# One V of each layer split by rows over five DMA engines: a two-layer decode kernel on one Trainium2 core

## Chip, core and metric

The kernel runs on one core of one Trainium2 chip. The metric is the device time of one execution in microseconds (us), as the median of the runs. Before the change it is 511.55 us, over 3 runs from 511.38 to 511.69.

## What is computed

One token of 640 numbers goes through two layers, and both layers use the same weights and the same caches:

```
x = x + A(layernorm(x))       # attention of one query over the last 4096 keys
x = x + B(layernorm(x))       # a mixer: two steps with a GELU in between
...
def A(x):
    q = (x @ wq).reshape(32 heads, 192)
    scores = q . k[last 4096 keys] * 192 ** -0.5        # per head
    p = softmax(scores)
    o = p . v[last 4096 keys]                           # per head, 192 numbers
    return o.reshape(6144) @ wo
```

Each of the 32 heads has a K and a V of 4096 x 192 bf16 numbers, 1.5 MB each, in HBM. (Of the reference's mixer B, the kernel computes what its output needs with one token.)

## The kernel before

**Layout.** A head's K or V lies in SBUF as 128 partitions of 32 keys each: partition p has the keys 32p to 32p + 31 in one row of 12,288 bytes. The 32 places in a row are called key blocks here. SBUF holds twelve such tiles, the cells (`take` and `give`, L147 to L153), and a few smaller places: `kx` (14 key blocks wide), `kl` (10), `wx_sb`, `wq_sb`.

**The stream of loads.** `layer_stream` (L247) writes down the order of all loads by hand, and `need` (L291) issues them on SP's queue in that order, in the place where the program first asks for a later one. In the steady part the K of the next group of four heads and the V of the present group take turns, and a part of `wo` follows each group. Layer 0 takes the groups from the last heads to the first, layer 1 from the first to the last. Some heads' data stay in SBUF between the layers: the transposed K of heads 0 to 7, and the V of heads 2, 3 and part of 4. `kx` and `kl` hold parts of the V of head 4 from late in layer 0 until its use early in layer 1. After a layer's attention the mixer's weights W3 and W4 are loaded (`load_w3` L212, `load_w4` L224). SP waits before an issue until the cell is free and until the semaphore that the load will use is free again; eight semaphores go round.

**How a load is split.** A load runs on up to 16 DMA engines. `load_wide` (L49) reads four rows at a time, so that a K or V is 32 packets of 49,152 bytes, two for each engine. The plain form makes a packet of each row, eight for each engine.

**The work on a head.** `T` turns K on DVE (L450), `S` makes the scores on PE (L534). Per group `softmax_steps` (L551) makes the weights of all four heads and turns them, so that `PT` (L607) has the weight of key block j of partition p in row p. `pv` (L645) multiplies: 16 products of two key blocks each (L654), added up in four strips of PSUM; DVE then turns the sums (L661), and `o_fold` (L663) adds them up. `give` in `pv` (L660) frees the cell. The products with `wo` are added up in rows, `acc` and `q_row`, for which `row_space` (L424) picks a place: in layer 1 the start of `kx`.

**Ends of layers.** In the mixer, L1015 makes the products with W3 and L1062 those with W4; the layer's result needs both. Layer 1 begins with scores of the kept heads, which need no load. Its first loads (L156, at 281.7 and 289.5 us of the span) wait for cells that the end of layer 0 frees.

Of the kernel before, what the change touches and what calls it, by code (L numbers as in the profile page):

```python
# [10 lines left out]
F32 = mybir.dt.float32  # L11
U32 = mybir.dt.uint32
ACTF = mybir.ActivationFunctionType
ALU = mybir.AluOpType
AX = mybir.AxisListType
# [3 lines left out]
P = 128  # L19
# [13 lines left out]
NJ4, NGK, NM = 4, 8, 4  # L33
# [22 lines left out]
        name=nc.get_next_instruction_name(), ins=sym[:1], outs=sym[1:], queue="qSPDynamicHW", mode="Copy"))  # L56


@with_exitstack
def kernel(  # L60
    ctx: ExitStack,
# [13 lines left out]
    nc = tc.nc  # L75
    shrink_ring(nc)
    _, _, D = A_x.shape
    _, H, Sk, Dh = A_k_cache.shape
# [9 lines left out]
    QH = 4  # L88
# [5 lines left out]
    FREE = NT * QUART  # L94
    scale = float(Dh) ** -0.5
    eps = 1e-5
    s0 = Sk - W

    NA = Dh // 32
    NKX, NKL = 14, 10  # L100
# [5 lines left out]

    VC, VP, VX, VW, VN = 3, 2, 4, 20 * Dh // 2, (NKL + NKX) * Dh
    assert NA * D + FREE - 2 * VW <= FREE

    W3C, W4C = FREE // F, FREE // D  # L110
    assert W4C % 2 == 1 and NF - W4C == 3
# [6 lines left out]
    kl = low.tile([P, NKL * Dh], BF16, name="kl")  # L118
# [9 lines left out]
    psm = ctx.enter_context(tc.tile_pool(name="psm", bufs=2, space=PSUM))  # L128
# [5 lines left out]
        name=nc.get_next_instruction_name(), act_func_set_id=ACT_TABLE_SET, ins=[], outs=[]))  # L134

    wq_sb = fixed.tile([P, ND, HD], BF16, name="wq_sb")
    wx_sb = fixed.tile([P, (ND - W3C) * F + (NF - W4C) * D], BF16, name="wx_sb")

    kx = fixed.tile([P, NKX * Dh], BF16, name="kx")
# [7 lines left out]
    def take(key):  # L147
        i = free.popleft()
        cell_of[key] = i
        return (low if i == NCELL - 1 else cells).tile([P, FREE], BF16, tag=f"cell{i}", name=f"cell{i}")  # L150

    def give(key):
        free.append(cell_of.pop(key))  # L153

    def load(dst, src, wide=True):
        (partial(load_wide, nc) if wide else nc.sync.dma_start)(dst, src)  # L156
# [10 lines left out]
        return t  # L167

    def load_v(layer, h):
        t = take(("v", layer, h))  # L170
        src = A_v_cache[0, h, s0:Sk, :].rearrange("(p j) d -> p (j d)", p=P)
        cut = (2 * VW,) if h == VP else (FREE - VN, FREE - NKX * Dh) if h == VX else ()
        if h in GROUPS[layer][-1][-1 - layer:]:
            cut = FREE // 2,
        i = 0
        for e in cut + (FREE,):
            kept_v = h == VP or h == VX and i > 0
            if not cut:
                load(t[:], src, layer == 0 or h >= 2)
            elif layer == 0 or not kept_v:  # L180
                nc.sync.dma_start(v_pair(t, h, i, e - i), src[:, i:e])
            i = e
        return t

    def v_pair(V, h, i, n):
# [105 lines left out]
    def need(*key):  # L291
        while key not in loaded:
            k = stream[pos[0]]
            pos[0] += 1
            loaded[k] = LOADERS[k[0]](*k[1:])
        return loaded[key]
# [3 lines left out]
    ident = const.tile([P, P], F32, name="ident")  # L300
# [3 lines left out]
    o_sb = big.tile([P, 2, NA, 32], F32, name="o_sb")  # L304
# [3 lines left out]
    def column(n):  # L308

        i = used[0]  # L310
        used[0] += n
        return words[:, i:i + n]
# [12 lines left out]
    def short_bf16(name, n, bufs=1):  # L325
        return short(name, (n + 1) // 2, bufs).bitcast(BF16)[:, 0:n]
# [3 lines left out]
        out=ident[:], in_=ident[:], compare_op=ALU.not_equal, fill=1.0,  # L330
# [7 lines left out]
    for base in (0, -1, -64, -65):  # L338
        nc.gpsimd.affine_select(
            out=Lf, in_=Lf, compare_op=ALU.not_equal, fill=1.0,  # L340
# [6 lines left out]
    Ei = ident[:].bitcast(BF16).rearrange("p (c two) -> p c two", two=2)[:, :, 1]  # L347
# [12 lines left out]

    Lq = head.tile([P, 32], F32, name="Lq")
    nc.vector.reduce_sum(Lq[:], ident[:].rearrange("p (j a) -> p a j", j=4), axis=AX.X)
    eps1 = column(1)
    nc.vector.memset(eps1[:], eps)

# [8 lines left out]
    QAT = 0, QPAIR, QPAIR + 2 * NM, NM  # L374
    Qblk = const.tile([P, 2, QSLOT], BF16, name="Qblk")
    nc.gpsimd.memset(Qblk[:], 0.0)


    warm_ps = psm.tile([32, 32], F32, tag="psm")
    for i in range(WARM):  # L380
# [9 lines left out]
                            op1=ALU.add, accum_out=rs0[:, 0:1])  # L390
# [32 lines left out]

    def row_space(layer):  # L424

        t, i = ((wx_sb, 8 * P), (kx, 0))[layer]
        return t[0:33, i:i + D].bitcast(F32), t[0:33, i + D:i + D + QC // 2]

    kept = {}
# [201 lines left out]
    O_ps = O_bank[:, 0:2 * Dh]  # L631
# [3 lines left out]
    def v_words(layer):  # L635

        V = need("v", layer, VP)
        step = 512
        for i in range(0, VW, step):
            n = min(step, VW - i)  # L640
            a = V[:, 2 * i:2 * (i + n)].bitcast(U32)
            b = V_bank[:, i:i + n].bitcast(U32)
            nc.vector.transpose(b if layer == 0 else a, a if layer == 0 else b)  # L643

    def pv(layer, h, hq, PT, mid=None):  # L645
        V = need("v", layer, h)
        if (layer, h) == (0, VP):
            v_words(0)
        NB = NJ4 * NGK // 2
        for i in range(NB):  # L650
            if mid is not None and i == NB // 2:
                mid()
            r = 32 * (i % 4)
            nc.tensor.matmul(O_ps[r:r + 2, :], lhsT=PT[:, hq, 2 * i:2 * i + 2],  # L654
                             rhs=v_pair(V, h, 2 * i * Dh, 2 * Dh), start=(i < 4), stop=(i >= NB - 4))
        if (layer, h) == (0, VC):
            loaded["v", 1, h] = V
            cell_of["v", 1, h] = cell_of.pop(("v", 0, h))
        else:
            give(("v", layer, h))  # L660
        nc.vector.transpose(o_sb[:], O_ps.rearrange("p (e a c) -> p e c a", e=2, c=NA))  # L661
# [64 lines left out]
    def attention(layer, x_cur, rs_cur, x_new, z_new, rs_new, ss_new):  # L726
# [54 lines left out]
        def center_y():  # L781
            y.pop()()
# [25 lines left out]
        early = None  # L808

        acc, q_row = row_space(layer)  # L810
        rows = range(2 * layer, len(groups) - 3 + layer)

# [6 lines left out]
        for gi, cur in enumerate(groups):  # L819
# [4 lines left out]
            quick = hurry and layer == 1  # L824
            ST_n = None
            if nxt:
# [3 lines left out]
                if layer == 1 and gi == 0:  # L830
# [17 lines left out]
                    PT = swap()  # L848
# [4 lines left out]
                else:  # L853
# [19 lines left out]
                    if layer == 1:  # L873
                        turn_p()
                        PT = swap()
# [16 lines left out]
                    if layer == 0:  # L892
                        PT = swap()
# [5 lines left out]
            else:  # L899
                PT, rl = early  # L900
            oT = short_bf16("oT", NA, 2)
            fold = None
            order = list(enumerate(cur))
            if layer == 1 and gi == 0:
                order.insert(0, order.pop(cur.index(VC)))
            for hq, h in order:
                if quick and hq == 1:
                    (q2, h2), (q3, h3) = nxt
                    T(h2, 0)
                    T(h2, 1)  # L910
                elif quick and hq == 2:
                    T(h3, 1)
                elif layer == 1 and nxt and 0 < hq < 3:
                    T(nxt[0][1], 0)
                pv(layer, h, hq, PT, steps[3] if quick and hq == 3 else fold)
                if final:
                    if hq == 0:
                        add_y(out_proj(layer, pending) if layer == 0 else turn_row(acc), 1)
                    if hq == 1:
                        center_y()  # L920
                    fold = None
                    if hq < QH - 2:
                        o_fold(h, oT, rl)
                    else:
                        def fold(h=h):
                            o_fold(h, oT, rl)

                    continue
                if quick and hq == 1:
                    S(h2, 0, ST_n, q2)  # L930
                    S(h2, 1, ST_n, q2)
                    T(h3, 0)
                elif quick and hq == 2:
                    S(h3, 0, ST_n, q3)
                    o_fold(h, oT, rl)
                    S(h3, 1, ST_n, q3)
                    steps = softmax_steps(len(cur), ST_n, sc, kl[:].bitcast(F32), V_bank)
                    for step in steps[:3]:
                        step()
                    continue  # L940
                elif hurry and hq == 1:
                    (q2, h2), (q3, h3) = nxt
                    for half in range(2):
                        T(h2, half)
                        S(h2, half, ST_n, q2)
                    T(h3, 0)
                    S(h3, 0, ST_n, q3)
                    T(h3, 1)
                elif hurry and hq == 2:
                    S(h3, 1, ST_n, q3)  # L950
                    steps = softmax_steps(len(cur), ST_n, sc, o_words)
                    steps[0]()
                    steps[1]()
                elif nxt and not (hurry and hq == 3):
                    q2, h2 = nxt.pop(0)
                    for half in range(2):
                        T(h2, half)
                        S(h2, half, ST_n, q2)
                o_fold(h, oT, rl, len(groups) - 4 > gi >= 2 * layer)
                if hurry and hq == 3:  # L960
                    for step in steps[4 if quick else 2:5]:
                        step()
                    early = steps[5](), steps[6]()
# [154 lines left out]
```

## Time and profile before

| | |
|---|---|
| median of 3 runs | 511.55 us |
| profiled execution | 511.54 us |
| its span, first to last instruction | 509.7 us |
| PE, DVE, ACT, POOL busy | 61%, 57%, 10%, 1% of the span |
| bytes moved by DMA | 214.63 MB, 421 GB/s on average |
| chain that ended last: share of DMA | 60% |
| a V's load, from issue to landing (median) | 27.7 us |

The profile is of one execution. The span leaves out what lies around it, here 1.8 us, so a change of so many us in the span is one of as many in the time. In the chain, each piece is what the next one waited for, followed back from the end. In groups of instructions the columns are the line, the engine, the operation, what it writes and reads, the shapes and the number, then busy us and the mean ns of one, then the idle time before them and who ended it. A queue's row has packets, megabytes and the share of 16 engines' time that the packets took.

### The profile page before, as it was taken

Reading aid. Unit: us, or ns where it says so; the run is one execution under the profiler, and the core shown is the slowest. Engines: PE = TensorE matmul, PEld = TensorE weight load, DVE = VectorE, ACT = ScalarE, POOL = GpSimd, SP = SyncE. Lnnn points to the kernel's source line nnn. Section 1 sums busy time; section 2 is a strip of 40 time slices with the busy share of each in tenths; the row PEclk is TensorE's granted clock in tenths of the full one; section 3 lists DMA queues with packets and bytes.
Section 4 is the critical chain, followed back from the end, with each engine's and each line's share of the span. In section 5 each row is a group of like instructions: output and inputs, shape, how many; then the busy total and the mean of one; then the engine's idle time right before and its main releaser. Section 6 shows DMA issues by size and latency. Waiting matters only on the chain.

```text
span 509.7 us, 9498 instructions
## 1 busy us (share of the span) xinstructions
PE 313.2 (61%) x4084; PEld 186.2 (37%) x4084; DVE 292.6 (57%) x604; ACT 48.9 (10%) x173; POOL 3.7 (1%) x16
## 2 busy tenths in 40 slices
PE   1056667666565555857655766767655765557685
PEld 0023333343332322534333643544322433324354
DVE  2067557666674755566723244968666656656522
ACT  1000101010010100001010101010100101001101
POOL 2000000000000000000000000000000000000000
PEclk9999756777597766576765586789887766857655
DMA  8999999999999999999999999999999999999996
GB/s 370 432 432 429 430 441 432 429 429 422 417 426 441 432 425 446 432 402 458 429 391 413 381 438 424 439 429 429 426 429 433 429 430 432 418 437 429 418 409 250
DMA packets 12014, 214.63 MB, mean 421 GB/s; under 512 B 2564, under 2 KB 3076, under 8 KB 7428
## 3 DMA queue, kind: packets, MB, share of 16 engines
q1 hardware_dynamic: 11972, 214.02, 98.5%
q8 instruction: 32, 0.52, 0.4%
q14 instruction: 10, 0.08, 0.0%
HBM read 214.01 MB, written 0.00 MB: 420 GB/s over the span
## 4 chain that ended last, share of the span: by engine, by line
DMA 60%; PE 20%; DVE 14%; issue 4%; ACT 1%; SPq 1%; DVEq 0%; ACTq 0%
DMA cell<-in_A_k_cache_dram 37%; DMA cell<-in_A_v_cache_dram 19%; DVE cell L450 9%; PE ST_ps L534 9%; PE O_ps L654 5%; DMA cell<-in_B_w_dram 4%; DVE o_sb L661 2%; PE qT_ps L480 1%; PE y_ps L1062 1%; PE nb_ps L580 1%; DVE words L557 1%; PE l_ps L613 1%; DVE V_ps L643 1%; DVE o_sb L591 1%; SPq L55 0%
## 5 line engine op out<-in xcount | busy, mean ns | idle before, releaser
L534 PE MATMUL ST_ps<-cell,Qblk 128*16 128x256 bf16 x1536 | 157.8, 364 | 110.8 <-DVE cell L450 66.6
L450 DVE STREAM_TRANSPOSE cell<-cell 128x768 uint32<-128x768 uint32 x224 | 201.6, 946 | 33.7 <-DMA cell<-in_A_k_cache_dram 31.6
L534 PEld LDWEIGHTS <-Qblk 128*16 128x16 bf16 x1536 | 84.7, 108 | 175.1 <-issue 150.2
L654 PE MATMUL O_ps<-cell,PT 128*2 128x384 bf16 x1000 | 90.2, 436 | 11.0 <-DMA cell<-in_A_v_cache_dram 9.1
L661 DVE STREAM_TRANSPOSE o_sb<-O_ps 128x384 f32<-128x384 f32 x64 | 36.7, 573 | 79.6 <-PE O_ps L654 79.5
L654 PEld LDWEIGHTS <-PT 128*2 128x2 bf16 x1024 | 41.2, 96 | 26.9 <-issue 18.7
L669 ACT ACTIVATE words<-oT_ps,words 32x6 bf16<-32x6 f32 x40 | 10.3, 257 | 163.6 <-PE oT_ps L668 150.3
L591 DVE STREAM_TRANSPOSE o_sb<-o_sb 128x256 bf16<-128x256 bf16 x15 | 6.7, 445 | 31.9 <-ACT o_sb L586 14.2
L668 PE MATMUL oT_ps<-o_sb,Lq 128*32 128x6 f32 x160 | 13.4, 192 | 10.7 <-DVE o_sb L661 10.1
L668 PEld LDWEIGHTS oT_ps<-o_sb,Lq 128*32 128x32 f32 x160 | 11.6, 137 | 20.4 <-issue 14.4
L674 ACT ACTIVATE words<-oT_ps,words 32x6 bf16<-32x6 f32 x24 | 6.2, 257 | 107.6 <-PE ST_ps L534 79.6
L480 PE MATMUL qT_ps<-words,wq_sb 128*128 128x1 bf16 x210 | 7.2, 165 | 12.9 <-DMA wq_sb<-in_A_wq_dram 12.0
L494 DVE TENSOR_TENSOR o_sb<-qT_ps,words 128x24 bf16<-128x24 f32 (+1 forms) x18 | 2.9, 163 | 20.2 <-PE qT_ps L480 17.4
L583 ACT COPY o_sb<-nb_ps 128x1 f32<-128x1 f32 x15 | 2.4, 159 | 102.2 <-PE nb_ps L580 102.2
L480 PEld LDWEIGHTS <-wq_sb 128*128 128x128 bf16 x210 | 6.8, 104 | 14.1 <-DMA wq_sb<-in_A_wq_dram 13.1
L605 PEld LDWEIGHTS <-ident 128*32 128x32 bf16 x256 | 5.8, 111 | 14.8 <-issue 14.5
L469 PE MATMUL qr_ps<-wq_sb,words 128*1 128x384 bf16 x90 | 10.7, 376 | 0.0
L700 PE MATMUL yr_ps<-cell,words 128*1 128x320 bf16 x108 | 10.4, 335 | 0.0
L673 PE MATMUL oT_ps<-o_sb,Lq 128*32 128x6 f32 x48 | 5.9, 194 | 6.8 <-DVE o_sb L672 6.8
L580 PEld LDWEIGHTS nb_ps<-words,o_sb 1*128 1x128 f32 x30 | 7.0, 287 | 7.2 <-issue 5.4
L673 PEld LDWEIGHTS oT_ps<-o_sb,Lq 128*32 128x32 f32 x48 | 5.0, 134 | 11.2 <-issue 9.1
L580 PE MATMUL nb_ps<-words,o_sb 1*128 1x1 f32 x30 | 8.2, 339 | 1.5 <-DVE o_sb L572 1.5
(159 smaller groups left out, 200.3 us busy)
## 6 DMA issues: line engine op xcount, KB each, us to landing
cell<-in_A_k_cache_dram SPq DMA_DIRECT2D x56, 1536.0 KB, 27.7
cell<-in_A_v_cache_dram SPq DMA_DIRECT2D x56, 1536.0 KB, 27.7
cell<-in_A_wo_dram SPq DMA_DIRECT2D x13, 960.0 KB, 27.5
wq_sb<-in_A_wq_dram SPq DMA_DIRECT2D x5, 1536.0 KB, 13.4
cell<-in_A_v_cache_dram SPq DMA_DIRECT2D x6, 768.0 KB, 23.7
cell<-in_B_w_dram SPq DMA_DIRECT2D x1, 1536.0 KB, 11.8
cell<-in_B_w_dram SPq DMA_DIRECT2D x2, 768.0 KB, 10.3
cell<-in_A_wo_dram SPq DMA_DIRECT2D x3, 480.0 KB, 17.0
```

Of the source, the lines that this page charges most:

```text
L450: nc.vector.transpose(Tu, Ku[:, :, q * NY:(q + 1) * NY])
L469: nc.tensor.matmul(qr_ps[32 * i:32 * i + 1, :], lhsT=xc[:, kc:kc + 1], rhs=wq_sb[:, kc, t0 * P + i * N:t0 * P + (i + 1) * N], start=(kc == ...
L480: nc.tensor.matmul(qT_ps[:, tl:tl + 1], lhsT=wq_sb[:, kc, t * P:(t + 1) * P], rhs=xc[:, kc:kc + 1], start=(kc == 0), stop=(kc == ND - 1))
L534: nc.tensor.matmul(ST_ps[r:r + QW, :].rearrange("p (g i) -> p g i", g=ng), lhsT=Q[n], rhs=T4[:, :, f, :, t], start=(hq == 0 and n == 0), s ...
L580: nc.tensor.matmul(nb_ps[:], lhsT=held["w"], rhs=one[0:1, :], start=True, stop=True)
L591: nc.vector.transpose(held["PrT"], held["Pr"])
L654: nc.tensor.matmul(O_ps[r:r + 2, :], lhsT=PT[:, hq, 2 * i:2 * i + 2], rhs=v_pair(V, h, 2 * i * Dh, 2 * Dh), start=(i < 4), stop=(i >= NB - 4))
L661: nc.vector.transpose(o_sb[:], O_ps.rearrange("p (e a c) -> p e c a", e=2, c=NA))
L668: nc.tensor.matmul(oT_ps[r, :], lhsT=Lq[:], rhs=o_sb[:, e, :, e], start=(e == 0), stop=(e == 1))
L669: nc.scalar.activation(oT[r, :], oT_ps[r, :], ACTF.Copy, scale=rl[r, 0:1])
L673: nc.tensor.matmul(oT_ps[r, :], lhsT=Lq[:], rhs=o2, start=True, stop=True)
L700: nc.tensor.matmul(yr_ps[32 * i:32 * i + 1, :], lhsT=oT[:, k:k + 1], rhs=wo_t[:, k * D + i * N:k * D + (i + 1) * N], start=(k == 0), stop= ...
```

## The change

One V of each layer, that of head 17 (`VM = QH * 4 + 1`), is loaded by a function of its own. The first 26 key blocks of all rows come in one plain load of 128 rows of 9,984 bytes. The last six key blocks (2,304 bytes a row) come in five loads more. Of rows 0 to 47 they go to their usual place: rows 0 to 19 in a load of five parts, rows 20 to 31 in one of twelve, rows 32 to 47 in one of four. Those of rows 48 to 127 go to `kx`, two rows beside each other in a partition: rows 48 to 87 to partitions 0 to 19, rows 88 to 127 to partitions 32 to 51, each a load of five parts. The weights have to follow: `deal_p` picks the weights of the moved rows with four small products and copies them to `kx` behind the data, and zeros the rows 20 to 31 in between by a factor (`dealt`). `pv_moved` then multiplies in 13 products over 128 rows, 3 over 48 rows and 6 over the 52 rows of `kx`, 22 in place of 16. Since `kx` is now used in layer 1, `row_space` takes its place from `kl` there.

```diff
+def load_rows(nc, dst, src, parts, u=1):
+    split = src.rearrange("(e r) n -> e r n", e=parts)
+    dst = dst.rearrange("p (u n) -> p u n", u=u)
...
+    VM, MB, ME, MU = QH * 4 + 1, 6, 5, 2
+    MR, MN = 4 * ME, MB * Dh
+    M0 = P - 2 * MU * MR
...
     def load_v(layer, h):
+        if h == VM:
+            return load_moved(layer, h)
...
+    def load_moved(layer, h):
+        t = take(("v", layer, h))
+        src = A_v_cache[0, h, s0:Sk, :].rearrange("(p j) d -> p (j d)", p=P)
+        nc.sync.dma_start(t[:, 0:FREE - MN], src[:, 0:FREE - MN])
+        for a, b, parts in (0, MR, ME), (MR, 32, 32 - MR), (32, M0, (M0 - 32) // 4):
+            load_rows(nc, t[a:b, FREE - MN:], src[a:b, FREE - MN:], parts)
+        for half in range(2):
+            a = M0 + MU * MR * half
+            load_rows(nc, kx[32 * half:32 * half + MR, 0:MU * MN], src[a:a + MU * MR, FREE - MN:], ME, MU)
+        return t
...
+    dealt = column(1)
+    nc.vector.reduce_sum(dealt, ident[:, MR:32], axis=AX.X)
+    nc.vector.tensor_scalar(out=dealt, in0=dealt, scalar1=-1.0, scalar2=1.0, op0=ALU.mult, op1=ALU.add)
...
+    nc.gpsimd.memset(kx[0:32, 0:MU * MN], 0.0)
...
-        t, i = ((wx_sb, 8 * P), (kx, 0))[layer]
+        t, i = ((wx_sb, 8 * P), (kl, 5 * P))[layer]
...
+    def deal_p(hq, PT):
+        Pm_ps = psm.tile([32 + MR, MU * MB], F32, tag="psm")
+        for half in range(2):
+            for u in range(MU):
+                a = M0 + MU * MR * half + u
+                m = 32 if half == 0 else MR
+                nc.tensor.matmul(Pm_ps[32 * half:32 * half + m, u * MB:(u + 1) * MB],
+                                 lhsT=Ei[:, a:a + MU * (m - 1) + 1:MU],
+                                 rhs=PT[:, hq, NJ4 * NGK - MB:], start=True, stop=True)
+        Pm = kx[:, MU * MN:MU * (MN + MB)]
+        nc.scalar.activation(Pm[0:32 + MR, :], Pm_ps[:], ACTF.Copy, scale=dealt[0:32 + MR, :])
+        return Pm
+
+    def pv_moved(layer, h, hq, PT, Pm):
+        V = need("v", layer, h)
+        NB = NJ4 * NGK
+        terms = [(PT[:, hq, i:i + 2], V[:, i * Dh:(i + 2) * Dh]) for i in range(0, NB - MB, 2)]
+        terms += [(PT[0:M0, hq, i:i + 2], V[0:M0, i * Dh:(i + 2) * Dh]) for i in range(NB - MB, NB, 2)]
+        terms += [(Pm[0:32 + MR, i:i + 2], kx[0:32 + MR, i * Dh:(i + 2) * Dh]) for i in range(0, MU * MB, 2)]
...
+            if VM in cur:
+                Pm = deal_p(cur.index(VM), PT)
...
-                pv(layer, h, hq, PT, steps[3] if quick and hq == 3 else fold)
+                if h == VM:
+                    pv_moved(layer, h, hq, PT, Pm)
+                else:
+                    pv(layer, h, hq, PT, steps[3] if quick and hq == 3 else fold)
```

More of the change, by code (lines that the diff above doesn't have):

```diff
@@ L54, in load_wide @@
     sym = [mybir.BassSymbolicTensorAccessPattern(ap=a.ap, dtype=a.dtype, bass_ap=a) for a in (wide, dst)]
+    return nc.sync.add_instruction(mybir.InstDMACopy(
+        name=nc.get_next_instruction_name(), ins=sym[:1], outs=sym[1:], queue="qSPDynamicHW", mode="Copy"))
+def load_rows(nc, dst, src, parts, u=1):
+    split = src.rearrange("(e r) n -> e r n", e=parts)
+    dst = dst.rearrange("p (u n) -> p u n", u=u)
+    sym = [mybir.BassSymbolicTensorAccessPattern(ap=a.ap, dtype=a.dtype, bass_ap=a) for a in (split, dst)]
     return nc.sync.add_instruction(mybir.InstDMACopy(
@@ L108 @@
     assert NA * D + FREE - 2 * VW <= FREE
+    VM, MB, ME, MU = QH * 4 + 1, 6, 5, 2
+    MR, MN = 4 * ME, MB * Dh
+    M0 = P - 2 * MU * MR
+    assert MB % 2 == 0 and MU * (MN + MB) <= NKX * Dh and M0 == 48
     W3C, W4C = FREE // F, FREE // D
@@ L643, in v_words @@
             nc.vector.transpose(b if layer == 0 else a, a if layer == 0 else b)
+    def deal_p(hq, PT):
[16 more added lines that the diff above has]
+        terms += [(Pm[0:32 + MR, i:i + 2], kx[0:32 + MR, i * Dh:(i + 2) * Dh]) for i in range(0, MU * MB, 2)]
+        for i, (p, v) in enumerate(terms):
+            r = 32 * (i % 4)
+            nc.tensor.matmul(O_ps[r:r + 2, :], lhsT=p, rhs=v, start=(i < 4), stop=(i >= len(terms) - 4))
+        give(("v", layer, h))
+        nc.vector.transpose(o_sb[:], O_ps.rearrange("p (e a c) -> p e c a", e=2, c=NA))
     def pv(layer, h, hq, PT, mid=None):
```

## The prediction, made before the changed kernel ran

> **What bounds the kernel now.** I read the page from the top: the slices, the queues, the chain; then the chain in order of time, the waits of the DMA queue (SP), the costs by shape in the stretch 120 to 180 us, and last the records under the trace, which hold start, length and size of each DMA packet and the 16 marks of each landing. All times below are us from the start of the span.
>
> ```profile
> DMA  8999999999999999999999999999999999999996
> ...
> q1 hardware_dynamic: 11972, 214.02, 98.5%
> q8 instruction: 32, 0.52, 0.4%
> q14 instruction: 10, 0.08, 0.0%
> ```
>
> The 16 DMA engines are busy in every slice. Nothing but the time of an engine's own packets counts: 3,616 packets of 49,152 bytes have a median of 1.820 us, whether or not the others run. The second and third queue are small in bytes; they fetch instructions, and they decide which engine is late.
>
> ```profile
> 273.72 10.01 DMA cell<-in_B_w_dram
> 283.73 0.05 issue
> 283.77 1.89 PE y_ps L1062 x60
> ...
> 492.52 10.31 DMA cell<-in_B_w_dram
> 502.83 0.05 issue
> 502.88 0.49 PE V_ps L1015 x12
> ```
>
> Both layers end by waiting for a landing: the mixer's W4 at 283.73, and the second half of W3 at 502.84. A landing is that of the slowest of 16 engines. Every engine has the same bytes, yet the 16 marks of that W3 piece lie, after the first one at 499.90, at 0.12, 0.13, 0.40, 0.54, 0.86, 0.88, 1.72, 1.76, 2.53, 2.62, 2.70, 2.71, 2.75, 2.81 and 2.94 us.
>
> To see who is late I linked packets to engines: on one engine the next packet begins 3 to 4 ns before the last one's end, so sixteen chains come out, up to swaps of engines that run within 1 ns. The load of x has five rows, and its five packets of 256 bytes mark five chains: I call these **the five**. Three things follow.
> - The 16 KB fetches (q8) go round eight other engines, and each sets its engine back by some 1.5 us (at 39.3 us one falls from 0.5 to 2.0 behind the first). These eight are the late half above.
> - The 8 KB fetches (q14) land on the five. One of the five, **engine A**, gets those at 51.5, 139.4 and 241.8, and each sets it back 0.88 to 0.91 (0.03 to 0.91, to 1.82, to 2.73 behind the first). Two others of the five get one each (0.3 to 0.6), two none.
> - In layer 1, A gets those at 327.9, 409.8 and 497.3: each time the engine then first, or nearly, falls back 0.9. A is the mark at 1.72 in W3's list: 1.22 ahead of the last, not 2.94.
>
> The queue is short of work for a moment only, between 282.1 and 293.6 (12 engine-us in all). A does not pause there: its last packet of W4 is followed at once by V of head 0 (284.25), and the next V at once by K (291.60).
>
> **The change, part by part.** *Packets.* Before, a V costs an engine 2 x 1.820 and a completion packet of 0.009: 3.65. Now the first load has 8 rows of 9,984 bytes; between 7,680 bytes (0.291) and 12,288 (0.460) that is 0.375 each, 3.00 plus 0.01. A row of 2,304 bytes lies between 1,280 (0.055) and 2,560 (0.102): 0.0925. The five loads of rows give the first four of the five engines 4 + 1 + 4 + 8 + 8 = 25 rows, the fifth 21, seven others one and four none. So:
> - first four: 3.01 + 25 x 0.0925 + 5 x 0.009 = 5.37, **1.72 more** per V
> - fifth: 3.01 + 21 x 0.0925 + 0.04 = 4.99, 1.34 more
> - the rest: 3.11 or 3.01, 0.53 or 0.64 less.
>
> That the loads of rows stay on the five that had x rests on their shape (five parts), as x had five rows; no row shows such a load. [...]
>
> *End of layer 0.* A's mark for the W4 piece (L233) is 282.94, the last one's 283.73. With 1.72 more A lands at 284.66; the eight late ones come 0.5 earlier. So the mixer waits 0.93 longer, and the loads behind it (the K at 289.5 waits for scores) are issued later by as much. A has no pause before and, being later, none now: it carries the whole 1.72 into layer 1. The others wait for the later K and lose there what they had won.
>
> *Layer 1.* The V of head 17 adds 1.72 again. A: 499.90 + 1.72 + 3.44 = 505.06 for W3, against 502.84: **2.22 later**. Check of the next: the eight late ones finish the V before that K at some 291.7, 0.5 early, wait to some 293.5 (the engines that paused there began at 292.6; 0.93 later) where they began at 292.2, +1.3, then gain 0.6 in layer 1: +0.7. The rest of the five: at most 0.88 + 0.93 + 1.72 = 3.53 against 2.94, +0.6. So A is last by over 1 us. From W3's landing to the end everything is the same work.
>
> *PE, ACT.* 13 + 3 + 6 = 22 products instead of 16, and four small ones and a copy once a layer:
>
> ```profile
> L654 PE MATMUL O_ps<-cell,PT 128*2 128x384 bf16 x115 | 10.7, 407 | 0.0
> ...
> L605 PE MATMUL PT_ps<-o_sb,ident 128*32 128x32 bf16 x32 | 0.9, 238 | 1.4 <-DVE wx_sb L710 1.4
> ```
>
> 6 x 0.41 + 4 x 0.24 + 0.27 (the copy like L608) = 3.7 per layer. Products over 48 or 52 rows are not in the trace; between nothing and 0.41 each, I take the full row. Queued behind them are the head's DVE transpose (L661, 0.58) and the next head. Cover: the loads. In these groups PE is busy 11.4 of 20 us, and loads are issued 27.7 before they land. I cost it at nothing; without that cover 3.7 per layer.
>
> *SP.* One issue becomes six, 5 x 0.47 more, and here lies the real danger:
>
> ```profile
> SPq L55 <- DMA cell<-in_A_v_cache_dram: 41.8, 13, 4.3
> SPq L55 <- DMA cell<-in_A_k_cache_dram: 40.3, 13, 3.4
> ```
>
> Between 355 and 460 SP waits 82 of 105 us for landings: eight semaphores go round, so eight loads are out (27.7 is 7.6 times 3.64). With six of the eight spent on one V, the K behind it is issued when the V before the V of head 17 has fully landed. The first engine then has K (3.64) and the first load (3.01) before it, less its lead of 2 to 3: 3.6 to 4.6 left. From issue to packet the pauses above show 1.8 (281.7 to 283.5) to 3.1. No pause, by 0.5 to 2.8. I take nothing.
>
> *The rest.* A memset of POOL and two DVE steps at the start (up to 0.4 and 0.3, as L557 and L572): DVE's first transpose waits for K until 25.1, and the V that needs the zeros is issued at 118.6. Rows in kl in place of kx: the same copies (L474, 0.47). The sixteen products over kx wait for the last loads of rows, issued up to 18 after the first but still ahead of it in the engines' queues. Nothing.
>
> **Sum.** 2.2 on the profiled execution of 511.54 (span 509.7), which stands at the median of 511.55: 513.7, 0.4% slower.
>
> **Rivals.**
> - *A is the fifth engine.* Then 2 x 1.34: W3 at 504.30, +1.46, 513.0. Nothing in the trace orders the five reliably; one in five by count.
> - *The first 1.72 is absorbed* in the gap between the layers. Only 1.72 + 1.72 = 3.44 against 2.94 is left: +0.5, and the others' +0.7 bound it: 512.2. Against it: A shows no pause there to absorb anything.
> - *The loads don't keep to five engines* (twenty rows over ten): ten engines then have 12 rows, 0.52 more per V. A stays ahead of the last (1.72 + 1.04 against 2.94), but two of the ten may be late ones, up to 1.0 later: 511.6 to 512.6, say 512.1.
> - *Other side, faster: A isn't one of the loaded five*, or its fetches move. Then the eight late engines set both ends, with 0.53 less per layer and no pause: 1.1 earlier, 510.4; the loaded five lose most of the first 1.72 in the gap and come to 0.54 + 1.72 + some 0.3 = 2.6 less the 0.5 of an earlier start, 0.8 earlier: say 510.6 (to 511.0 if one relief is lost). It decides as long as the latest of the five carries less than 1.2 into W3. For it: it is the plain reading, five engines of which none takes a 16 KB fetch. Against: A's x packet and its five falls of 0.9.
> - *The queue runs dry* behind the six loads: the margin of 0.5 to 2.8 fails and all engines pause 1 to 2 per layer, on top of the forecast: 514.4 to 517.5, say 515.5.
>
> **Numbers.** Forecast (A one of four, 513.2 to 514.3) 0.48, A the fifth 0.14, dry 0.11, absorbed 0.08, ten engines 0.04, other side 0.15. About 0.2%, 1.0 us, is what a measurement of this kernel can tell from no change: slower 0.48 + 0.14 + 0.11 = 0.73; within 0.08 + 0.04 and 0.02 of the other side = 0.14; faster 0.13. The range 510.9 to 514.8 leaves out most of the other side (0.13) and the worse part of a dry queue (0.07).
>
> **What would show it.** In the profile after: W4 of layer 0 landing near 284.7 and W3 near 505.1, with one engine alone at the back by some 1 us; the loads of rows as five small entries per layer in the issues; DMA digits of 9 behind the V of head 17 (a lower one there is the dry queue); L661 not later by more than its loads. Wrong: if the last mark before W4 comes earlier than 283.7, the engine at the back is none of the five, and the other side holds.

## The result

The changed kernel takes 514.08 us, the median of 6 runs (513.73 to 514.77), against 511.55 (511.38 to 512.05, 6 runs) for the kernel before on the same chip: a ratio of 1.005, with a 95% interval from 1.0037 to 1.0063. It is slower by some 2.5 us. Its profiled execution took 513.93 us with a span of 512.1, so 2.4 more than that of before on either count.

### The profile page after: what moved, and what is told of

The parts are those of the page before. It is cut to its first block, busy times and chain, and to the rows that moved or that the text cites. A ratio compares the mean times of both kernels' runs of the same rounds, so it can differ in the third digit from the quotient of the medians.

```text
span 512.1 us, 9561 instructions
## 1 busy us (share of the span) xinstructions
PE 311.8 (61%) x4104; PEld 185.3 (36%) x4104; DVE 293.0 (57%) x606; ACT 49.5 (10%) x175; POOL 5.7 (1%) x17
## 4 chain that ended last, share of the span: by engine, by line
DMA 55%; PE 20%; DVE 18%; issue 3%; ACT 1%; SPq 1%; DVEq 0%; ACTq 0%
DMA cell<-in_A_k_cache_dram 32%; DMA cell<-in_A_v_cache_dram 19%; DVE cell L483 12%; PE ST_ps L567 8%; PE O_ps L713 5%; DMA cell<-in_B_w_dram 4%; DVE o_sb L720 2%; PE qr_ps L502 1%; PE nb_ps L613 1%; PE y_ps L1126 1%; DVE words L590 1%; DVE o_sb L624 1%; PE PT_ps L638 1%; DVE V_ps L676 1%; ACT o_sb L619 1%
## 5 line engine op out<-in xcount | busy, mean ns | idle before, releaser
L567 PE MATMUL ST_ps<-cell,Qblk 128*16 128x256 bf16 x1536 | 155.2, 361 | 111.8 <-DVE cell L483 66.0
L713 PE MATMUL O_ps<-cell,PT 128*2 128x384 bf16 x968 | 88.0, 434 | 9.9 <-DMA cell<-in_A_v_cache_dram 7.9
L720 DVE STREAM_TRANSPOSE o_sb<-O_ps 128x384 f32<-128x384 f32 x62 | 35.5, 573 | 78.8 <-PE O_ps L713 78.8
```

Source lines behind the costliest of these rows:

```text
L567: nc.tensor.matmul(ST_ps[r:r + QW, :].rearrange("p (g i) -> p g i", g=ng), lhsT=Q[n], rhs=T4[:, :, f, :, t], start=(hq == 0 and n == 0), s ...
```

## The profile after

The page, in the same order: the DMA slices and the queues (packets, megabytes, share of 16 engines' time).

```profile
DMA  8999999999999999999999999999999999999994
...
q1 hardware_dynamic: 12482, 214.02, 98.2%
q8 instruction: 32, 0.52, 0.4%
q14 instruction: 10, 0.08, 0.0%
```

The same bytes and the same number of instruction fetches, in 510 packets more. The queue was full in every slice but the first and the last; there the digit fell from 6 to 4: most engines are done while one is still at work (the marks below). The bytes are the same, so the time is to be looked for in how they are shared out.

The chain of waits at the two ends, in order of time (start, length, what):

```profile
274.64 9.96 DMA cell<-in_B_w_dram
284.60 0.05 issue
284.64 1.96 PE y_ps L1126 x60
```

```profile
494.03 11.14 DMA cell<-in_B_w_dram
505.17 0.05 issue
505.21 0.49 PE V_ps L1079 x12
```

These are the pieces shown of before with 283.73 and 502.83 in the second line (L1062 and L1015 are now L1126 and L1079). The mixer of layer 0 starts 0.87 later, and the second half of W3 lands 2.34 later. From there to the end nothing is new: the output lands at 511.07 where it landed at 508.73, again 2.34.

The sixteen marks of that W3 piece say who was late. After the first at 499.77 they lie at 0.18, 0.26, 1.56, 1.58, 1.71, 1.76, 2.11, 2.27, 2.54, 2.60, 3.33, 3.33, 3.63, 4.02 and 5.39 us. Before, seven stood within 0.41 of each other at the back. Now one engine stands alone, 1.37 behind the next. The loads by rows show which: in layer 0 the marks of the five-part load over rows 0 to 19 lie at 0, 0.13, 0.14, 0.17 and 2.00, and those of the four-part load at 0, 0.09, 0.11 and 1.91. One of the loaded engines is already 2 us behind the others, and the load of four parts has one such as well.

At the end of layer 0 no engine stands alone like that: the last mark of W4 is at 284.60 and the next at 284.30. That is one of the late engines, which lost 1.2 us around 268 us (a pause of 0.71 and a packet of 7,680 bytes that took 813 ns in place of 291); all others are before 283.3.

The new packets took what was worked out: 93 ns (median) for 2,304 bytes, 375 for 9,984. Two views show what hid the rest. First the products and the copy, by shape, in the stretch 119 to 180 us (line, engine, operation, output and input, shape, number, then busy us and mean ns):

```profile
L713 PE MATMUL O_ps<-cell,PT 128*2 128x384 bf16 x92 | 10.2, 469 | 0.0
...
L700 PE MATMUL O_ps<-kx 52*2 52x384 bf16 x6 | 0.6, 322 | 0.0
L641 ACT CAST PT<-PT_ps 128x128 bf16<-128x128 f32 x2 | 0.5, 266 | 5.8 <-PE PT_ps L638 5.8
L689 ACT ACTIVATE kx<-Pm_ps,words 52x12 bf16<-52x12 f32 x1 | 0.3, 266 | 1.7 <-PE Pm_ps L685 1.7
```

The six products over `kx` found their data there: the 0.0 at the end is PE's idle time before them. Then SP's waits between 355 and 460 us (in all, times, longest):

```profile
SPq L55 <- DMA cell<-in_A_v_cache_dram: 33.3, 11, 3.1
SPq L55 <- DMA cell<-in_A_k_cache_dram: 29.8, 10, 3.1
SPq L64 <- DMA cell<-in_A_v_cache_dram: 6.1, 2, 3.3
SPq L64 <- DMA cell<-in_A_k_cache_dram: 5.6, 2, 2.8
```

The row loads (L64) wait for landings like any other, and the K behind the six is issued at 139.09, where the load behind that V was issued at 122.2 before. Yet, counted from the packets in steps of 0.5 us, at least 15.6 of the 16 engines were busy throughout 108 to 165 us and 359 to 419 us: no pause behind the split V. A short one lies elsewhere, before the change too: around 266 us the distance of A to the first engine falls from 2.74 to 1.95 us before and from 4.40 to 3.02 after. The first engines lost 0.8 and 1.4 us there, and A lost nothing: its two marks are 2.29 apart before and 2.30 after.

## The experiments

**First theory (engine A).** An engine's own packets alone count. The row loads put 1.72 us per V on four engines, one of them is A, which three 8 KB fetches per layer had set back already, and A's landing is the end of both layers after the change. **Second theory (loads).** Six loads on eight semaphores, or six issues, cost the time. **Third theory (products).** The longer work on the head costs it. Twelve kernels ran, in three groups; the kernel before took 511.9 (511.54 to 513.27), 511.62 (511.25 to 512.28) and 511.77 (511.26 to 513.94) beside them.

### One layer alone

```diff
-        if h == VM:
+        if h == VM and layer == 0:      # second kernel: layer == 1
             return load_moved(layer, h)
```

and the same condition for `deal_p` and `pv_moved`.

> Only layer 0's V of head 17 is split over the five engines; layer 1 loads it and multiplies it as before the change. Theory 1 (engine A, one of the five, which also takes the 8 KB instruction fetches, is set back 1.72 us and sets the end of layer 0; layer 1 then begins 0.93 later): W4 of layer 0 lands near 284.6, A reaches W3 at 499.9 + 1.72 + 1.72 = 503.3, and the eight late engines, without the relief in layer 1, at some 504.3; so 1.4 over before, 513.0. Theory 2 (six loads hold six of eight semaphores, the queue runs short and each such V costs the same): half of the 2.5, 512.8. Theory 3 (six more products and the dealing on PE): half as well, 512.8. It is the pair with the next kernel that tells them apart.

> Only layer 1's V of head 17 is split over the five engines. Theory 1: the end of layer 0 stays where it was (W4 at 283.7), A reaches W3 at 499.9 + 1.72 + 1.72 = 503.3, the late eight at 502.3; 0.5 over before, 512.0. Theories 2 and 3: half of the 2.5, 512.8, the same as with layer 0 alone.

Layer 0 alone: 513.57 us, ratio 1.0034 [1.0021, 1.0047]. Layer 1 alone: 512.18, ratio 1.0005 [0.9996, 1.0014]. The chain's two landings in the first:

```profile
274.85 10.02 DMA cell<-in_B_w_dram
...
494.55 10.30 DMA cell<-in_B_w_dram
504.85 0.05 issue
```

and the second one's at the end of layer 1:

```profile
492.61 10.88 DMA cell<-in_B_w_dram
503.49 0.05 issue
```

The same loads, issues and products cost 1.7 in layer 0 and 0.3, not to be told from nothing, in layer 1. Two theories that count them alike for each layer do not fit that. The first had the two in this order, since A's distance to the last one is spent only once: 0.8 at the end of layer 0, 1.2 at the end of layer 1. In size layer 0 missed by half a us (W4 at 284.87 for 284.6, W3 at 504.85 for 504.3), and layer 1 hit (503.49 for 503.3). Layer 0 is here the same program as in the changed kernel, where W4 landed at 284.60: a landing differs by some 0.3 us between two executions, and a closer agreement than that says little.

### The products alone

```diff
-        if h == VM:
-            return load_moved(layer, h)
...
-    nc.vector.tensor_scalar(out=dealt, in0=dealt, scalar1=-1.0, scalar2=1.0, op0=ALU.mult, op1=ALU.add)
+    nc.vector.tensor_scalar(out=dealt, in0=dealt, scalar1=0.0, scalar2=0.0, op0=ALU.mult, op1=ALU.add)
...
-        terms += [(PT[0:M0, hq, i:i + 2], V[0:M0, i * Dh:(i + 2) * Dh]) for i in range(NB - MB, NB, 2)]
+        terms += [(PT[:, hq, i:i + 2], V[:, i * Dh:(i + 2) * Dh]) for i in range(NB - MB, NB, 2)]
```

> The V of head 17 is loaded as before the change, in one wide load, but its products are those of the change in number: four small ones, a copy and 22 in place of 16, the six more over kx with weights of zero. First theory: 511.7, as before. Second (loads): 511.7 as well. Third (products and the wait for them): 514.1.

It took 511.54, ratio 0.9999 [0.9991, 1.0008]. The work is there, by shape over the whole span:

```profile
L687 ACT ACTIVATE kx<-Pm_ps,words 52x12 bf16<-52x12 f32 x2 | 0.5, 266 | 4.6 <-PE Pm_ps L683 4.6
L698 PE MATMUL O_ps<-kx 52*2 52x384 bf16 x12 | 1.1, 378 | 0.0
```

and it costs nothing. The third theory is out, and the products are hidden, as the prediction had it.

### The number of loads

Two kernels keep V whole and split the last six key blocks into five pieces, first by rows, then by columns:

```diff
+        nc.sync.dma_start(t[:, 0:FREE - MN], src[:, 0:FREE - MN])
+        for a, b in (0, 32), (32, 64), (64, 96), (96, 112), (112, 128):
+            nc.sync.dma_start(t[a:b, FREE - MN:], src[a:b, FREE - MN:])
```

```diff
+        nc.sync.dma_start(t[:, 0:FREE - MN], src[:, 0:FREE - MN])
+        for i in range(FREE - MN, FREE, 256):
+            e = min(i + 256, FREE)
+            nc.sync.dma_start(t[:, i:e], src[:, i:e])
```

> Six loads for that V in both layers, with the same first load and the same 2,304-byte rows, but each of the five small ones goes evenly over 16 engines and all rows lie in their usual place; products as before the change. Theory 1: each engine gets 3.01 + 8 x 0.0925 + 0.045 = 3.80 instead of 3.65, 0.15 per V: 511.85. Theory 2: as slow as the changed kernel, 514.1. Theory 3: 511.55.

> The kernel before, but the V of head 17 in six loads: the first 26 key blocks as in the change, the last six in five pieces of columns (four of 512 bytes, one of 256) over all 128 rows and all 16 engines; nothing is moved and no product is added. First theory (engine A carries the most bytes and sets both ends): every engine gets the same, 40 short packets of some 27 ns in place of 0.64 us, 0.5 more per V and 0.9 to 1.0 in all: 512.5, no pause. Second theory (six loads on eight semaphores, or six issues, cost the time): as the change or more, 514.1 to 515. Third (the products): 511.7.

By rows: 516.22, ratio 1.008 [1.0067, 1.0093]; all three theories missed. By columns: 512.07, ratio 1.0008 [0.9999, 1.0017]. So six loads, short packets included, cost 0.45 us here, and 0.9 at the upper end of the interval (the first theory had put 0.9 to 1.0 on the short packets alone), and the second theory is out as the cause of 2.5. The kernel by rows shows something else. It had no pause either, but its packets were slow: those of 2,304 bytes took 120 ns in the mean (96 in the changed kernel), those of 9,984 bytes 412 (379), and even the 49,152-byte ones of the neighbours were stretched while the pieces ran, to 2.8 us at most in place of the usual 1.82 (the longest of before took 2.42, beside an instruction fetch).

### A third of the bytes, and one load more

```diff
-    VM, MB, ME, MU = QH * 4 + 1, 6, 5, 2
+    VM, MB, ME, MU = QH * 4 + 1, 2, 5, 2
```

> The change with two key blocks moved in place of six (rows of 768 bytes, first load of 11,520 bytes a row): the same six loads, engines, products over kx fewer by four. By packets in proportion (768 bytes 0.037, 11,520 bytes 0.431) A has +0.77 per V: 283.7 at W4, level with the late ones, and 503.2 at W3 against 502.7 for them. First theory (A pays only what exceeds its distance of before): 511.9. Theory of the six loads: as the change, 514.1. A cost in proportion to the bytes on the five: 0.45 of the change's 2.4, 512.7.

It took 511.96, ratio 1.0007 [0.9996, 1.0018], with the same six loads of the same parts; the packets took 36 and 432 ns. 1.54 us more on A cost 0.2, where 3.44 cost 2.5: a cost that begins only once A's distance is used up, as the first theory has it. (The profiled execution happened to be one of 514.0 us, so its landings are not used here.)

```diff
-        for a, b, parts in (0, MR, ME), (MR, 32, 32 - MR), (32, M0, (M0 - 32) // 4):
+        for a, b, parts in (0, MR, ME), (MR, 32, 32 - MR), (32, 36, 2), (36, 48, 3):
```

> The changed kernel, but the rows 32 to 47 of the last six key blocks come in a load of two parts (4 rows) and one of three parts (12 rows) instead of one of four. The landing marks of these tell where engine A is: it shows as a mark some 2 us behind the others of its load. Theory 1: it is among the first four, by the four-part load of the changed kernel; a mark 2 us behind in the three-part load puts it among the first three, in the two-part load among the first two. Time as the changed kernel's, 514.0, by all theories (one look).

A single run took 515.35, span 513.5, where every theory had 514.0. It bears on where A is. In layer 0 the five-part loads show one engine 2.0 to 2.3 behind, the three-part load shows 0, 0.03 and 0.11, the two-part load 0 and 0.07. No run names the engine of a packet; on the assumption that a load of fewer parts takes the first of the same engines, A is in the first four and not in the first three: it is the fourth. The seventh load also did what six did not. The stretch 398 to 404 us (busy us of each engine, then PE's clock, DMA share, GB/s), here and in the changed kernel:

```profile
398.00:404.00 6.00, 3.96 (x51) 2.41 (x50) 2.84 (x6) 2.02 (x6) 0.00 (x0) 0.90 0.91 341
```

```profile
398.00:404.00 6.00, 4.11 (x45) 2.23 (x42) 3.25 (x7) 1.55 (x5) 0.00 (x0) 0.50 1.07 447
```

Counted from the packets in steps of 0.5 us, the number of engines at work fell to 2.8 of 16 within that stretch: the queue ran dry. The rival of the dry queue was one load away.

### The same load without A, and with it

If A is the cause, the same rows on three engines should cost little. Three kernels tried that. The first puts the tails of rows 0 to 79 in one load over 16 engines and rows 80 to 127 on three; the second gives rows 0 to 79 to ten engines instead; the third gives rows 0 to 63 to eight and rows 64 to 127 to four, so that A, as the fourth, has what the first three have.

```diff
-    VM, MB, ME, MU = QH * 4 + 1, 6, 5, 2
+    VM, MB, ME, MU = QH * 4 + 1, 6, 3, 2          # third kernel: 4
...
-        for a, b, parts in (0, MR, ME), (MR, 32, 32 - MR), (32, M0, (M0 - 32) // 4):
-            load_rows(nc, t[a:b, FREE - MN:], src[a:b, FREE - MN:], parts)
+        load_rows(nc, t[0:M0, FREE - MN:], src[0:M0, FREE - MN:], 16)      # then M0 // 8
```

> The change with three engines in place of five: rows 0 to 79 keep their tail, in one load over 16 engines, and rows 80 to 127 go to 24 partitions of kx in two loads of three parts; four loads in all, and two small products more to deal the weights. The first three engines then have 21 short rows per V (+1.2), all others 5 (-0.28), engine A among them. First theory: both ends come 0.3 and 0.6 earlier than before the change, if the first three keep ahead: 511.2, at most 512.0, and not one engine alone at the back by over 1 us. Second theory (loads): four loads, so some half of the change's loss, 512.9. Third (products): all of it, 514.1.

> The change with three engines in place of five, and no row on a foreign engine but on those: the tails of rows 0 to 79 in one load of ten parts (eight rows each), those of rows 80 to 127 in two loads of three parts to kx. The first three engines then have 24 short rows per V, +1.6; the fourth, A, has 8, +0.1; the last six have none, -0.6. First theory: A (501.62 + 0.2) and the late ones among the ten (502.84 + 0.2) set the second end, the first three come to at most 3.2 to 3.6 behind the first of before against 2.94: 511.8 to 512.2. Rival (any loaded engine, or any load by rows, costs the time, not A): as the next kernel, 513.4. That the slow packets of the earlier kernel with three engines come from rows 0 to 79 over 16 engines: here, with each row on the engine that has it in the first load, the short packets keep to 93 ns.

> As the kernel with three engines and own rows, but with four: the tails of rows 0 to 63 in one load of eight parts, rows 64 to 127 in two loads of four parts, 16 rows for each engine as there. What changes beside it is that A, the fourth engine, is one of those with 24 rows (+1.6 per V). First theory: A at W4 at 282.94 + 1.6 = 284.55 and at W3 at 501.62 + 3.2 = 504.8, alone at the back: 513.5, some 1.5 more than with three. Rival (not A): the same time as with three engines.

They took 512.78 (ratio 1.0023 [1.0014, 1.0032]; one of its eleven runs took 521.95), 513.88 (1.0037 [1.0023, 1.0052]) and 515.12 (1.0062 [1.0046, 1.0077]). Every one is above what the first theory gave, by 1.6 to 2.1. But the last two differ as it said: A in the loaded set costs 1.2 more (1.5 expected), and no run of the one reaches those of the other (513.04 to 514.31, 514.81 to 515.38). The chain's landing of W3, with three and with four engines:

```profile
495.29 10.33 DMA cell<-in_B_w_dram
505.62 0.05 issue
```

```profile
495.36 11.17 DMA cell<-in_B_w_dram
506.53 0.05 issue
```

With three, the last mark is 0.29 behind the next. With four it stands alone, 1.92 behind. The difference comes in layer 1. W4 of layer 0 landed at 285.32 with three engines and at 285.49 with four, where the theory had A make the difference at that end too (284.55 with four). With three, the engine that ends layer 0 is one that a 16 KB fetch at 245.5 us set back by 1.55. What all three kernels have beyond the theory is again slow packets: 106, 112 and 113 ns for 2,304 bytes. The row order that was meant to keep each row on its own engine did not prevent it; no trace names the rows of a packet, so whether it kept them there is not shown. (The relief of 0.28 per V expected of the first kernel is wrong as well: 3.01 + 5 x 0.0925 + 0.009 = 3.48 against 3.65 is 0.17. With it the expectation would be some 0.2 higher, 511.4, and still missed.)

### Slow packets by themselves

```diff
+        nc.sync.dma_start(t[:, 0:FREE - MN], src[:, 0:FREE - MN])
+        for a in 0, 64:
+            nc.sync.dma_start(t[a:a + 64, FREE - MN:], src[a:a + 64, FREE - MN:])
```

> The kernel before, with the V of head 17 in three loads: the first 26 key blocks, then the tails of rows 0 to 63 over all 16 engines, then those of rows 64 to 127 over all 16; nothing moved, no product added, the same bytes on each engine. First theory alone (only an engine's bytes count): 0.1 per V, 511.8, all short packets at 93 ns. Theory of the crowded partitions (packets become slow where 16 engines write into half the partitions): some 1.2 per V and engine, as with the loads of 32 rows: 514, with short packets at 115 to 125 ns in the mean and the 9,984-byte ones above 400.

515.94, ratio 1.0078 [1.0063, 1.0093]: the same bytes on each engine, three loads, nothing moved, and 4.2 us slower. Short packets took 133 ns, the 9,984-byte ones 425. The stretch 144 to 148 us of this kernel, of the one with three engines and ten parts, and of the one by columns:

```profile
144.00:148.00 4.00, 2.39 (x39) 1.45 (x39) 3.92 (x8) 0.79 (x3) 0.00 (x0) 0.86 1.24 368
```

```profile
144.00:148.00 4.00, 1.62 (x27) 1.27 (x26) 3.92 (x8) 0.56 (x2) 0.00 (x0) 0.79 1.05 361
```

```profile
144.00:148.00 4.00, 2.25 (x47) 1.51 (x50) 3.89 (x12) 0.27 (x1) 0.00 (x0) 0.94 1.30 529
```

The last two numbers are the share of DMA and its GB/s. The engines are just as busy, and move 361 to 368 GB/s where the kernel by columns, whose pieces all span 128 partitions, moves 529. In so short a stretch the rate depends on which packets fall into it, since whole packets are counted, and 529 is far above that kernel's mean. Over 140 to 148 us the halves move 366 GB/s and three engines 378, against 444 by columns, 438 in the changed kernel and 470 before.

How far this explains the misses can be worked out. I add up by how much the packets around the two V loads exceed 93, 375 and 1,821 ns, divide by 16 engines, and add it to the W3 landing that the bytes alone give (502.83 plus 0.3 by rows in five pieces, 0.2 in halves, less 0.34 with 16 parts, plus 0.2 with ten; 504.84 for A with four engines):

| kernel | by bytes | slow packets, per engine | sum | measured |
|---|---|---|---|---|
| changed kernel | 505.06 | 0.22 | 505.28 | 505.17 |
| five pieces by rows | 503.13 | 3.65 | 506.78 | 506.91 |
| two halves | 503.03 | 3.54 | 506.57 | 507.08 |
| three engines, 16 parts | 502.49 | 1.58 | 504.07 | 503.65 |
| three engines, ten parts | 503.03 | 2.18 | 505.21 | 505.62 |
| four engines, eight parts | 504.84 | 1.62 | 506.46 | 506.53 |

Bytes per engine and slow packets together give each landing to about 0.5 us. The slow packets of the kernel by columns come to 0.06 by this count. Counted in the same way over 130 to 160 and 385 to 420 us, the kernel before has 0.17 and the changed kernel 0.25, so values of this size say nothing. The kernel with seven loads has 1.10, which with 505.06 would be 506.16; it landed at 506.55, but there the dry queue is mixed in.

### More steps on DVE

```diff
     def pv(layer, h, hq, PT, mid=None):
+        if layer == 0:
+            for _ in range(5):
+                nc.vector.memset(spare, 0.0)
```

> The change, with 155 steps more on DVE in layer 0 (five memsets of one column for each other head), to no use of their own. First theory, with the 8 KB fetches on engine A taken as those of DVE's instructions: one or two more of these packets, each 0.9 on A, and A still last: 515.0 or 515.9, and A's distance behind the next at W3 larger by the same. Rival (A is late for another reason, or its fetches are not DVE's): the same ten fetches and 514.1; if DVE itself is slower by its 155 steps, at most 9 us of busy time, the ends come later without a mark of A.

514.83, ratio 1.0064 [1.005, 1.0077]. The page counts one fetch more:

```profile
q14 instruction: 11, 0.09, 0.0%
```

A's series of 51.5, 139.4 and 243.5 us in the changed kernel became 49.9, 115.4, 180.7 and 250.0, while the other fetches of layer 0 (150.6 and 186.1, now 150.5 and 186.1) stayed. So with 155 more steps on DVE one more fetch fell on A, four in place of three. W4 landed 1.03 later and W3 1.18. But the first mark at W4 was later by 1.18 as well, and at W3 the last one stood 1.43 behind the next, hardly more than the 1.37 of the changed kernel, so that this part of the expectation failed. The time fits; that A alone carried it to the end is not shown.

## Why the prediction was right

The forecast was 513.7 and the time 514.08; in the profiled executions 2.2 was predicted and 2.4 measured. By its steps:

- **Packets.** 0.0925 and 0.375 us were predicted, 0.093 and 0.375 measured (medians). The sum of 1.72 per V rested on them. Late in layer 0 (the load whose first mark is at 264.98 in both kernels) A's mark is 1.66 later than before.
- **Which engines.** That the row loads take the same five engines each time, and that the first four of these get 25 rows, was an assumption from the shape: no run names the engine of a packet. The runs agree as far as they go: in layer 0 a five-part load has one engine 2.00 us behind and the four-part load one 1.91 behind, while the loads of three and of two parts have none more than 0.11 behind.
- **A is one of the first four.** This was a guess, as the prediction said: nothing in the trace of before orders the five. It had the most weight (0.48), and that it held is luck of four in five. The four-part load and the kernel with two- and three-part loads agree with it, if fewer parts mean the first of the same engines. The rivals "A is the fifth" and "other side, faster" fall with that.
- **End of layer 0.** A at 284.66 was predicted, 284.60 measured; the wait of 0.93 came out as 0.87. So close a hit is luck, given 284.87 for the same layer in another execution. "One engine alone at the back by some 1 us" did not come true here: by the prediction the late eight would land 0.5 earlier, at 283.2. All but one did, and that one landed at 284.30, 0.30 before A. The prediction also had the queue short of work between 282.1 and 293.6 only; around 266 us it is short too, and there as well A has no pause.
- **The first 1.72 is not absorbed.** W3 was predicted at 505.06 and landed at 505.17, with A alone at the back "by over 1 us": 1.37. A's own mark is 3.56 later than before (505.17 against 501.61), where 2 x 1.72 = 3.44 were worked out. With layer 1 alone W3 landed at 503.49; the 1.68 us more came with the V of layer 0.
- **Products, copy, start.** Nothing was predicted, and the kernel with the products alone shows nothing. The products over 52 rows took 0.32 us in layer 0, inside the bounds, and 0.51 in layer 1, above the 0.41 taken as the most (the products over 128 rows of the same V took 0.51 there as well). The memset of POOL took 2.0 us, not the 0.4 taken from smaller ones; it lies at the start, hidden all the same.
- **The queue does not run dry.** Right for six loads; with seven per V it ran dry. (The sum of this rival is off: 1 to 2 us per layer on top of 513.7 is 515.7 to 517.7, not 514.4 to 517.5.)

The small miss, 0.2 us in the profiled executions and 0.4 in the medians, is no larger than what the runs leave open (the interval of the ratio is 513.4 to 514.8 us), and no run shows a cause for it: the slow packets of the changed kernel are hardly more than those of the kernel before.

What the working lacked is a term for slow packets. It said that nothing but the time of an engine's own packets counts, whether or not the others run. The trace of before bears that out for the 2,560-byte packets, which took 102 ns (median) with fewer than eight engines at work and with all 16; its 49,152-byte ones all ran with 15 or more at work. In general it is wrong: the same 2,304-byte packets took 133 ns in the mean in the kernel with two halves, against 96 in the changed kernel. The change escapes this, and which part of its shape spares it no run shows; the prediction did not weigh it, so here it was lucky; five of the test kernels did not escape, and the sign came out wrong for one that I took to be faster than before (511.2 expected, 512.78 measured).

## What to carry to other kernels

When all transfer engines are busy throughout, work out the time of each engine, not the mean: the landing of W3 here came with the last of its 16 marks, 1.37 us behind the next, and an engine that instruction fetches have set back may have far less room than its neighbours (A was 1.22 us ahead of the last before the change, the first engine 2.94). Moving work to engines that are early pays only if none of those taken is near the back, and here the loads of four and five parts took one that was 2 us behind, those of two and three parts did not. When a load is cut by rows, look at the duration of its neighbours' packets as well: in the kernel with two halves the 9,984-byte packets of the first load took 425 ns, against 379 in the changed kernel.

## What was not expected of the hardware

- **Cutting a load by rows came with slow packets.** Cutting the last six key blocks of one V per layer into halves of 64 rows cost 4.2 us; the rate over 140 to 148 us fell to 366 GB/s, against 444 by columns, while all engines were busy. By the table the excess per engine and V was 1.77 us in halves and 1.82 in five pieces by rows, 0.79 and 1.09 with three engines (16 and ten parts), 0.81 with four and 0.11 in the changed kernel; by columns it was 0.03. The number of rows in a load does not order them: the loads of the changed kernel have 12 to 40 rows, and its excess is the least in the table. No trace says what a packet waits for, so the cause is not shown.
- **The row loads of the change are not slowed.** But for the load of twelve parts, each part is four neighbouring rows, or goes to four neighbouring partitions of `kx`, and the 2,304-byte packets kept to a median of 93 ns (96 in the mean). No run separates this order from there being only four or five writers.
- **The fetch that came with more steps on DVE fell on the late engine.** In layer 0, 155 steps more brought one more 8 KB fetch, in the series of the engine that was already last.
- **With seven loads for one V the queue ran dry.** With six, at least 15.6 of the 16 engines are busy behind the split V; with seven the number at work drops to 2.8 of 16 in layer 1, in one run.
